# The first step of a fused linear-attention and MoE kernel: loads by two queues, half chunks staggered, y cleared by TensorE

## The chip, the cores and the metric

The kernel runs on one NeuronCore of one Trainium2 chip. The metric is the time of one execution on the device, in microseconds (us). Engines are named as the profile names them: PE (TensorE; PEld is its weight load), DVE (VectorE), ACT (ScalarE), POOL (GpSimd) and SP (SyncE, which here only issues transfers). ACT issues a few transfers too.

## What is computed

Two blocks are chained. The first is an RWKV-6 attention with a decay for each channel and token; the second is a feed-forward block with the gate h * erf(softplus(h)).

```python
# r, k, v, w: (B, H, S, D) = (4, 8, 768, 48); u: (8, 48)
for t in range(S):
    cur = einsum('bhd,bhe->bhde', u * k_t, v_t)
    y_t = einsum('bhd,bhde->bhe', r_t, state + cur)
    state = w_t[..., None] * state + einsum('bhd,bhe->bhde', k_t, v_t)
x = y.transpose(0, 2, 1, 3).reshape(3072, 384)
h = x @ w_in                                   # 384 -> 2048
g = h * erf(maximum(h, 0) + log1p(exp(-abs(h))))
out = g @ w_out                                # 2048 -> 384
```

## The kernel before

The sequence is cut into 6 chunks of 128 tokens and the 4 batches into 2 pairs, which gives 12 steps; a step handles one chunk of two batches (called j = 0 and 1 below, or half 0 and half 1 of the step). Inside a step, heads lie in pairs on the partitions: 48 channels of one head on partitions 0 to 47 and of the other on 64 to 111, in 8 columns of 128 tokens (n = 0 to 3 belong to batch 0 and n = 4 to 7 to batch 1).

Attention inside a chunk is done by halving, on two blocks of 64 tokens. At level n (1 to 6) the products of k in the left half of each block of 2^n tokens with r in its right half are made on PE (`level_products`, the matmul at L701), into one of two pairs of PSUM banks, `pp0` and `pp1`, that take turns. `take_level` (L711 on DVE, L718 on ACT) or `take_blocks` (L732 on ACT, level 5) moves them to their places in `own`, the matrix of token pairs. `scale` (L357 for one half of step 0, L364 for a whole step) then multiplies the left halves of k and the right halves of r by the decays of the other half of their blocks, in place on DVE, so that the next level's products are right. These decays are products of w over blocks, `totals`, made on POOL at L386. So within one batch the order is: scale of level n-1, products of level n, scale of level n. A product bank is free again when its level has been taken. Level 1 also carries the token's own term: it reads `rk1`, a copy of r and k in which every second token is multiplied by u (L408 and L412 on DVE, L425 and L428 on ACT).

After level 6 k is transposed on PE (L1012) into the bank that held level 5, copied to `kT` (L1015, one half by DVE and the other by ACT), and `from_own` (L745) and `state_part` (L818) make the outputs y in PSUM and the state. `fence` (L754) is a small DVE read that separates the two passes of `from_own`. `middle` is copied (L1025 on ACT, L1026 on DVE), and `through_state` (L771) adds the part of y that comes through the state. For step 0, L786 and L792 then put y into `xT`, and the projections follow: `hidden` (L1231, w_in) and `project` (L1353, w_out).

Step 0 is `attend_first`. It has nothing else to run beside it except the first weight pieces: the weights arrive as 64-bit numbers in 16 pieces of two transfers of 384 KB each and are converted by `stages`: "l" loads (L181; it waits behind a one-element copy, L272 or L274, that times it), "b" is L289 on ACT, "r" is L297 on ACT, "h" is L306 on DVE, "o" is L319 on POOL. In later steps these stages lie between the levels. `load_second` (copy L211, transfers L181) loads r and k of step 1, and `prepare(1)` makes the `rk1` of step 1, r by ACT (L425, L428) and k by POOL (L417, L421). `wait_for` (L962) is a one-element POOL copy that keeps the totals behind a scale.

Everything from `load_first` on is in one region whose engine queues keep the order in which the code issues the instructions. An instruction that waits holds up everything behind it on its engine.

`stay_warm` (L1056) and `keep_busy` (L1065) are matmuls on the identity whose results nobody reads. Before the steps DVE clears `y`, `sums`, both product banks and `apart` (L1608 to L1614), and POOL clears the states (L1625).

Of the kernel before, what the change touches and what calls it, by code (L numbers as in the profile page):

```python
# [11 lines left out]
FP32 = mybir.dt.float32  # L12
# [5 lines left out]
P = 128  # L18
# [73 lines left out]
def kernel(  # L92
    ctx: ExitStack,
    tc: tile.TileContext,
    rkw: bass.AP,
    v: bass.AP,
# [90 lines left out]
    def load_first():  # L187
# [7 lines left out]
        )  # L195
        nc.scalar.dma_start(out=u_sb[:], in_=u)
        nc.sync.dma_start(out=t5[:, 0], in_=rkw[0][:, 0:2, b0])
        nc.sync.dma_start(out=t5[:, 1, 0], in_=rkw[0][:, 0, b1])
        nc.sync.dma_start(out=t5[:, 1, 1], in_=rkw[0][:, 1, b1])
        nc.sync.dma_start(out=ws[0][:, b0], in_=rkw[0][:, 2, b0])  # L200
        nc.sync.dma_start(out=ws[0][:, b1], in_=rkw[0][:, 2, b1])
# [165 lines left out]

    def plan_totals(s):
# [21 lines left out]
    def prepare(s):  # L390


        if s < DIRECT:
# [3 lines left out]
            parts = 1 if s else NJ  # L397
            def multiply_u(i, x):
                n = slice(i * JP // parts, (i + 1) * JP // parts)
# [3 lines left out]
                        for t in (rk1[:, x, n], in_t[:, x, n] if s else turns["first"][:, i, x])  # L403
# [3 lines left out]
                if not s and not (x and not i):  # L407
                    nc.vector.tensor_mul(  # L408
                        with_u[0], with_u[1],
                        u_sb[:, :, None].to_broadcast([P, NP, C // 2]),  # L410
                    )
                    nc.vector.tensor_copy(out=plain[0], in_=plain[1])  # L412
                    return
# [16 lines left out]
            if s < 2:  # L430
                for i in range(parts):
                    for x in range(2):
                        multiply_u(i, x)
                        yield
                return
            yield
            yield
            multiply_u(0, 0)
# [14 lines left out]
        if s < DIRECT:  # L453
            ready[s] = rk1, tots, tot
            yield
            yield
            multiply_u(0, 1)
            return
# [480 lines left out]
    def attend_first(xT):  # L939


        for _ in prepare(0):
            pass
# [3 lines left out]
        own = att.tile([P, NH, HC], FP32, name="own")  # L947
        halves = [range(j * NP, (j + 1) * NP) for j in range(NJ)]
        batch = JP * C // 2 // NJ
        pp = products([P, NE, JP, HC])  # L950
        for half in halves:
            level_products(pp, by_pair(made), 1, half)
            stay_warm(2)
        nc.scalar.copy(first[:], mask_sb[:, 0, :])
        totals(1, part=slice(0, batch))
        for j in range(NJ):
            scale(0, 1, batch=j)
        load_second(t5[:, 1, 0, NP - 1, 1:2])

        def wait_for(t):  # L960

            nc.gpsimd.tensor_copy(out=block_sb[:, 0:1], in_=t5[:, 1, 0, NP - 1, t : t + 1])  # L962

        wait_for(1)
        totals(1, part=slice(batch, 2 * batch))
        totals(2, part=slice(0, batch // 2))
        nc.vector.tensor_mul(
            own[:], pp[:].rearrange("p e n t -> p (e n) t"),
            first[:, None, :].to_broadcast([P, NH, HC]),
        )  # L970
        behind = {3: (3,), 4: (4, 5), 5: (6,)}
        for level in range(2, LOG):
            pp = turns.pop("pp", None) or products([P, NE, JP, HC])
            for j, half in enumerate(halves):
                level_products(pp, first_pair, level, half)
                scale(0, level, batch=j)
            turns["pp"] = products([P, NE, JP, HC])
            keep_busy(turns["pp"], (DM,))
            (take_blocks if level == MASKED else take_level)(own, pp, level)
# [12 lines left out]
            if level == 3:  # L992
                stages["l"](1, ready[0][1][level][:, 0:1])
# [813 lines left out]
```

## Time and profile before

| what | value |
|---|---|
| time, median of 3 runs | 570.8 us (570.66 to 571.3) |
| time of the profiled execution | 571.11 us |
| its span on the core | 569.3 us |
| PE busy | 561.7 us, 99% of the span |
| DVE, ACT, POOL busy | 449.6, 359.2, 245.7 us |
| step 0, start of the span to the first matmul of `hidden(0)` | 0 to 26.44 us |
| granted PE clock in every stretch asked for | 1.00 |

The span is the part that the profile sees; 1.8 us of the execution's time lie around it. A timeline line reads: start, length, engine, source line, operation, output<-input, shape, count, and in brackets how long the engine was idle before it and what released it. A line with a count merges neighbours, so its length is that of the whole run of them. A line of a table by stretches gives the stretch, its length, then busy time and number of instructions of PE, PEld, DVE, ACT and POOL, the granted PE clock, the share of the DMA engines and GB/s.

### The profile page before, as it was taken

The numbers are of one execution on the slowest core, as the hardware profiler recorded it, in microseconds if no ns is written. First come the engines' busy times: TensorE is split into PE (matmuls) and PEld (weight loads), VectorE is DVE, ScalarE is ACT, GpSimd is POOL, SyncE is SP. The second block draws the span as 40 slices with busy tenths as digits, with TensorE's granted clock in tenths as the row PEclk, the third lists the DMA queues.
The fourth block names the chain that finished last, engine by engine and source line by source line (L and its number), as shares of the span: only waits on it lengthen the run. The fifth ranks groups of instructions, "written<-read, shape, count | busy, mean of one in ns | idle before, by whom it ended". The sixth has DMA issues, their size and how long they took to land.

```text
span 569.3 us, 16709 instructions
## 1 busy us (share of the span) xinstructions
PE 561.7 (99%) x7318; PEld 500.2 (88%) x7318; DVE 449.6 (79%) x508; ACT 359.2 (63%) x495; POOL 245.7 (43%) x264
## 2 busy tenths in 40 slices
PE   8999999999999999999999999999999999999997
PEld 6788886688998998998998998898899899989997
DVE  8774886999899898799789689689688487477730
ACT  4668787655458858747756765766676771589500
POOL 3775481632885883383484175176073000000000
PEclk9999999999999999999999999999999999999999
DMA  8794762350435325155145236235332201000000
GB/s 272 241 355 161 249 200 86 151 162 3 147 80 174 109 74 155 33 166 164 31 143 181 39 123 200 39 112 167 48 112 84 47 9 36 2 2 1 28 29 28
DMA packets 54081, 63.24 MB, mean 111 GB/s; under 512 B 35160, under 2 KB 40568, under 8 KB 52984
## 3 DMA queue, kind: packets, MB, share of 16 engines
q1 hardware_dynamic: 53480, 61.98, 34.7%
q8 instruction: 57, 0.93, 0.7%
q10 hardware_dynamic: 528, 0.20, 0.1%
q14 instruction: 16, 0.13, 0.1%
HBM read 52.39 MB, written 8.69 MB: 107 GB/s over the span
## 4 chain that ended last, share of the span: by engine, by line
PE 77%; DVE 7%; issue 3%; POOL 1%; ACT 1%; DMA 0%; ACTq 0%; POOLq 0%
PE m L1353 33%; PE m L1231 27%; PE c L1456 6%; PE pp L701 3%; PE m L1263 2%; PE y L745 2%; DVE in L364 2%; PE y L771 1%; PE pp L818 1%; POOL w_out_sb L1294 1%; DVE h L1196 1%; DVE sums L569 1%; PE c L1353 0%; DVE words L503 0%; DMA xT<-y 0%
## 5 line engine op out<-in xcount | busy, mean ns | idle before, releaser
L1231 PE MATMUL m<-xT,w_in_sb 128*128 128x256 f32 x960 | 214.6, 381 | 0.4 <-ACT h L1240 0.2
L1231 PEld LDWEIGHTS m<-xT,w_in_sb 128*128 128x128 f32 x960 | 180.1, 190 | 25.5 <-issue 0.6
L364 DVE TENSOR_TENSOR in<-in,tot_sb 128x1024 f32<-128x1024 f32 (+1 forms) x55 | 75.3, 1370 | 8.9 <-PE pp L701 6.5
L1240 ACT COPY h<-m 128x512 f32<-128x512 f32 x80 | 46.3, 580 | 52.6 <-PE m L1231 52.2
L1353 PE MATMUL m<-mixed,h 128*128 128x192 f32 x320 | 56.7, 331 | 0.0
L1353 PE MATMUL m<-w_out_sb,h 128*128 128x192 f32 x320 | 56.1, 329 | 0.0
L1353 PEld LDWEIGHTS m<-mixed,h 128*128 128x128 f32 x320 | 51.8, 190 | 0.8
L1353 PEld LDWEIGHTS m<-w_out_sb,h 128*128 128x128 f32 x320 | 52.0, 190 | 0.5
L1353 PE MATMUL m<-w_out_sb,room 128*128 128x192 f32 x288 | 49.7, 326 | 0.0
L1353 PEld LDWEIGHTS m<-w_out_sb,room 128*128 128x128 f32 x288 | 47.3, 190 | 0.1
L503 POOL TENSOR_TENSOR words<-words,own 128x384 f32<-128x384 f32 x21 | 30.4, 1447 | 25.7 <-DVE words L534 13.0
L1191 ACT ACT_TABLE_LOAD x28 | 35.9, 1283 | 8.7 <-DVE h L1196 6.7
L701 PEld LDWEIGHTS pp<-in 48*48 48x48 f32 (+4 forms) x2368 | 30.1, 120 | 10.9 <-issue 6.0
L544 POOL TENSOR_TENSOR words<-words 128x384 f32<-128x384 f32 x28 | 38.7, 1410 | 0.0
L496 POOL TENSOR_TENSOR own<-rest 128x384 f32<-128x384 f32 x7 | 8.1, 1156 | 69.2 <-PE y L745 35.1
L1187 ACT ACT_TABLE_LOAD x28 | 35.9, 1283 | 1.8 <-issue 1.3
L701 PE MATMUL pp<-in 48*48 48x32 f32 (+4 forms) x2368 | 33.9, 206 | 0.3 <-DVE in L364 0.3
L448 POOL TENSOR_TENSOR tot_sb<-tot_sb 128x256 f32<-128x256 f32 (+4 forms) x50 | 31.6, 632 | 3.8
L569 DVE TENSOR_REDUCE sums<-rk 128x16 f32<-128x768 f32 (+2 forms) x31 | 31.4, 1023 | 0.0
L544 POOL TENSOR_TENSOR rk<-words 128x384 f32<-128x384 f32 x28 | 30.6, 1121 | 0.0
L1187 ACT ACTIVATE room<-h 128x1024 f32<-128x1024 f32 x28 | 29.6, 1057 | 0.3
L319 POOL TENSOR_TENSOR w_out_sb<-w_out_sb,rest 128x768 int32<-128x768 int32 x8 | 18.1, 2264 | 21.7 <-DVE w_out_sb L311 21.5
(218 smaller groups left out, 1008.1 us busy)
## 6 DMA issues: line engine op xcount, KB each, us to landing
in<-in_rkw SPq DMA_DIRECT2D x8, 1024.0 KB, 5.1
words<-in_moe_w_in SPq DMA_DIRECT2D x16, 384.0 KB, 5.6
words<-in_moe_w_out SPq DMA_DIRECT2D x16, 384.0 KB, 4.6
words<-in_rk_rows SPq DMA_DIRECT2D x8, 768.0 KB, 6.6
w<-in_rkw SPq DMA_DIRECT2D x11, 512.0 KB
v<-in_v SPq DMA_DIRECT2D x12, 384.0 KB, 5.6
out<-o SPq DMA_DIRECT2D x23, 192.0 KB, 4.1
in<-in_rkw SPq DMA_DIRECT2D x7, 512.0 KB, 5.8
```

What stands on the lines that cost most here:

```text
L364: nc.vector.tensor_mul(halves, halves, view(tots[level - 1], 0, [[1, n], [2, nb], [0, half]]))
L448: nc.gpsimd.tensor_mul(new, pair[:, :, 0], pair[:, :, 1])
L503: engine.tensor_mul(to, to, of[:, :, None, :].to_broadcast([P, NEAR // 2 // half, half, D]))
L544: engine.tensor_mul(to[:, i], r[:, half:], k[:, part * rows + i, None].to_broadcast([P, half, D]),)
L569: nc.vector.tensor_reduce(out=to, in_=of, axis=mybir.AxisListType.X, op=ALU.add)
L701: nc.tensor.matmul(to, lhsT=rk(1, n)[rows(e), s0 : s0 + m], rhs=right, start=True, stop=True,)
L1187: nc.scalar.activation(sp_room, chunks[0], AF.Softplus)
L1191: nc.scalar.activation(at, sp_room, AF.Erf)
L1231: nc.tensor.matmul(ps[:, ff, :], lhsT=w_in_sb[:, g * FG + f + ff, kk * P : (kk + 1) * P], rhs=xT[:, kk, :], start=kk == 0, stop=kk == KT - 1,)
L1240: nc.scalar.copy(h[:, f : f + FT, :], ps[:])
L1353: nc.tensor.matmul(to, lhsT=a[:, f], rhs=b[:, f], start=start and f == 0, stop=f == FG - 1, skip_group_check=True,)
L1456: nc.tensor.matmul(to[:, f], lhsT=turns["weights"][b][:, i * FT + f], rhs=turns["tokens"][a], start=a + b in STARTS and not f, stop=True, ...
```

## The change

Only step 0 and what stands before it are touched. The host also gives r, k and w of step 0 in an order that puts the two batches one after the other (`in_rkw_first`), so that a partition's r and k of one batch are one piece of 4 KB where they were two of 2 KB.

- First loads: r and k of batch 0 are loaded in two halves of 64 partitions, one by SP's queue and one by ACT's, followed on ACT's by `u`. Then SP loads w of batch 0, r and k of batch 1 in one transfer (two before), w of batch 1 and the masks.
- Before the steps: `load_first` moves into the ordered region, `y` is no longer cleared by DVE, `sums` and `apart` are cleared by POOL, and `stay_warm` runs 4 matmuls where it ran 6.
- Copies and products with u: r by DVE and k by ACT for both batches (before, k of batch 1 was DVE's too).
- Order: batch 0 runs one level ahead of batch 1. Level 1's products (`next_tokens`) are made after level 2's, and go to the two PSUM banks of the projections (`near`), so level 2 can start without them; `take_next_tokens` moves them in two DVE instructions before level 2 is taken.
- The matmuls that nobody reads between levels (L1065, and L1056 beside level 1) go. `clear_y` takes their places: 9 matmuls of 128 columns of zeros, which clear y.
- `scale_last` replaces the scale of level 6: k's halves first, for both batches, and r's only for the second 64 tokens of a chunk, after k's.
- Stages of the first weight piece: "l" is placed after the first total, "b" and "r" come after step 1's product with u on ACT (before them, earlier), and both "h" come ahead of the fence (one on each side before). The loads of the pieces 1 and 2 and of step 1's w wait behind other elements.

```diff
+        for queue, part in ((nc.sync, slice(0, EP)), (nc.scalar, slice(EP, P))):
+            queue.dma_start(out=t5[part, 0], in_=rkw_first[part, 0, 0:2])
         nc.scalar.dma_start(out=u_sb[:], in_=u)
-        nc.sync.dma_start(out=t5[:, 0], in_=rkw[0][:, 0:2, b0])
-        nc.sync.dma_start(out=t5[:, 1, 0], in_=rkw[0][:, 0, b1])
-        nc.sync.dma_start(out=t5[:, 1, 1], in_=rkw[0][:, 1, b1])
-        nc.sync.dma_start(out=ws[0][:, b0], in_=rkw[0][:, 2, b0])
-        nc.sync.dma_start(out=ws[0][:, b1], in_=rkw[0][:, 2, b1])
+        nc.sync.dma_start(out=ws[0][:, b0], in_=rkw_first[:, 0, 2])
+        nc.sync.dma_start(out=t5[:, 1], in_=rkw_first[:, 1, 0:2])
+        nc.sync.dma_start(out=ws[0][:, b1], in_=rkw_first[:, 1, 2])
         nc.sync.dma_start(out=mask_sb[:], in_=masks)
...
+    def scale_last(batch, k):
+
+        half, nb = 1 << (LOG - 1), JP * C // NJ >> LOG
+        t, tots = turns["first"][:, batch], ready[0][1]
+        at, every, of = (NP * C, 1, 1) if k else (half + HC, NC, 2)
+        halves = view(t, at, [[2 * half * every, nb // every], [1, half]])
+        nc.vector.tensor_mul(
+            halves, halves,
+            view(tots[LOG - 1], 2 * batch * nb + of, [[2 * every, nb // every], [0, half]]),
+        )
...
+        def plain(i):
+            to, of = every_second(i, 1, 0)
+            nc.scalar.copy(to, of)
+            to, of = every_second(i, 0, 1)
+            nc.vector.tensor_copy(out=to, in_=of)
+        def times_u(i):
+            to, of = every_second(i, 0, 0)
+            nc.vector.tensor_mul(to, of, u_sb[:, :, None].to_broadcast([P, NP, C // 2]))
+            to, of = every_second(i, 1, 1)
+            for p in range(NP):
+                nc.scalar.mul(out=to[:, p], in_=of[:, p], mul=u_sb[:, p : p + 1])
+        near = [ps_m.tile([P, NP * C], FP32, name="m") for _ in range(NE)]
+        near = [t[:].rearrange("p (n t) -> p n t", t=HC) for t in near]
...
+        def clear_y(times=2):
+            to = y[:].rearrange("p e q j t -> p (e q j) t")
+            zeros = states[1][0][:].rearrange("p n d -> p (n d)")[:, :C]
+            for _ in range(times):
+                nc.tensor.matmul(
+                    to[:, cleared["of"] % (NE * NP)], lhsT=ident[:], rhs=zeros,
+                    start=True, stop=True, skip_group_check=True,
+                )
+                cleared["of"] += 1
...
+        plain(0)
+        times_u(0)
+        scale(0, 1, batch=0)
+        level(pp, 2, 0)
+        next_tokens(0)
+        wait_for(0, 1)
+        totals_of(0, 1)
+        stages["l"](0, t5[:, 1, 1, NP - 1, C - 1 : C])
+        totals_of(0, 2)
+        clear_y(1)
+        plain(1)
+        times_u(1)
+        scale(0, 2, batch=0)
+        later_pp = products([P, NE, JP, HC])
+        level(later_pp, 3, 0)
+        scale(0, 1, batch=1)
+        level(pp, 2, 1)
+        next_tokens(1)
+        clear_y()
         nc.scalar.copy(first[:], mask_sb[:, 0, :])
...
         load_second(t5[:, 1, 0, NP - 1, 1:2])
+        nc.sync.dma_start(out=vt[:], in_=v[0])
+        wait_for(1, 1)
+        totals_of(1, 1, 2)
+        scale(0, 3, batch=0)
+        scale(0, 2, batch=1)
+        level(later_pp, 3, 1)
+        clear_y()
+        take_next_tokens()
+        take_level(own, pp, 2)
+        wait_for(1, 0, 2)
+        totals(3, 4, 5)
+        second = prepare(1)
+        next(second)
+        stages["b"](0, 0)
+        stages["b"](0, 1)
+        scale(0, 3, batch=1)
+        stages["l"](1, t5[:, 1, 0, NP - 1, 4:5], True)
+        stages["r"](0)
+        pp, later_pp = later_pp, products([P, NE, JP, HC])
+        level(later_pp, 4, 0)
+        scale(0, 4, batch=0)
+        level(later_pp, 4, 1)
+        clear_y()
+        take_level(own, pp, 3)
+        scale(0, 4, batch=1)
+        wait_for(1, 0, 8)
+        totals(6)
+        nc.gpsimd.tensor_copy(out=ws[1][:, 0, 0:1], in_=block_sb[:, 0:1])
+        nc.sync.dma_start(out=ws[1][:], in_=rkw[1][:, 2])
+        pp, later_pp = later_pp, products([P, NE, JP, HC])
+        level(later_pp, 5, 0)
+        scale(0, 5, batch=0)
+        level(later_pp, 5, 1)
+        clear_y()
+        take_level(own, pp, 4)
+        scale(0, 5, batch=1)
+        take_blocks(own, later_pp, 5)
         totals = plan_totals(1)
+        pp = products([P, NE, JP, HC])
+        for i in range(NJ):
+            level(pp, LOG, i)
+            scale_last(i, True)
         take_level(own, pp, LOG)
+        wait_for(0, 1)
+        stages["l"](2, block_sb[:, 0:1])
+        wait_for(1, 1)
         next(second)
+        for i in range(NJ):
+            scale_last(i, False)
...
         stages["h"](0)
+        stages["h"](0)
         fence()
-        stages["h"](0)
...
-    nc.vector.memset(y[:], 0.0)
-    nc.vector.memset(sums[:], 0.0)
...
-        stay_warm(6)
+        load_first()
+        stay_warm(4)
+        for t in banks:
+            nc.vector.memset(t[:], 0.0)
+        nc.gpsimd.memset(apart, 0.0)
```

The loop over levels 2 to 5 that this replaces is in the listing above.

## The prediction

> **What bounds the kernel now.** I read the table by stretches first, then the timeline of step 0, then the transfers.
>
> ```profile
> 5.00:10.60 5.60, 5.37 (x134) 3.99 (x133) 4.99 (x13) 2.34 (x8) 2.19 (x5) 1.00 0.97 318
> 10.60:19.60 9.00, 7.94 (x292) 5.24 (x284) 8.74 (x13) 5.69 (x13) 3.83 (x11) 1.00 0.77 253
> ...
> 26.40:60.00 33.60, 33.60 (x754) 27.89 (x746) 20.86 (x22) 24.70 (x42) 21.75 (x24) 1.00 0.66 239
> 60.00:569.30 509.30, 505.29 (x5956) 455.41 (x5954) 407.80 (x449) 321.11 (x423) 209.47 (x205) 1.00 0.31 95
> ```
>
> From 26.4 us PE never stops, so whatever moves the first projection matmul moves the end by as much; the change touches only what lies ahead. There, from 10.6 to 19.6, DVE is busy 8.74 of 9.00 us: it sets step 0, not PE.
>
> ```profile
> 5.00 1.08 ACT L425 ACTIVATE rk<-in,u_sb 128x64 f32<-128x64 f32 x4 [2.29 <-DMA in<-in_rkw]
> 5.00 0.43 DVE L408 TENSOR_TENSOR rk<-in,u_sb 128x256 f32<-128x256 f32 x1
> ...
> 7.09 1.71 DVE L357 TENSOR_TENSOR in<-in,w 128x512 f32<-128x512 f32 x2
> ...
> 9.06 0.81 SPq L181 DMA_DIRECT2D in<-in_rkw  x2
> ...
> 13.76 1.32 ACT L425 ACTIVATE rk<-in,u_sb 128x128 f32<-128x128 f32 x4 [1.24 <-DMA in<-in_rkw]
> ...
> 16.88 1.49 ACT L732 COPY own<-pp 16x256 f32<-16x256 f32 x4 [1.24 <-PE pp L701]
> ...
> 18.28 1.32 DVE L357 TENSOR_TENSOR in<-in,tot_sb 128x512 f32<-128x512 f32 x2 [0.24 <-POOL block_sb L962]
> ...
> 18.62 1.18 ACT L718 COPY own<-pp 32x512 f32<-32x512 f32 x2 [0.25 <-PE pp L701]
> ...
> 19.14 1.16 PE L1012 MATMUL pp<-ident,in 128*128 128x128 f32 x8 [0.59 <-DVE in L357]
> ...
> 21.00 0.48 ACT L1015 COPY kT<-pp 128x384 f32<-128x384 f32 x1 [1.21 <-DVE kT L1015]
> ```
>
> The chain: r and k of batch 0 land just before 5.0; DVE works through to 19.60; the second four transposes wait for its last scale; then the kT copies (to 21.48) and `through_state` at 23.18. ACT has slack: between its product with u (13.76) and the blocks of level 5 (16.88) it idles 1.24 us, waiting for PE. That slack is what the change spends, below.
>
> ```profile
> GB/s 0 0 0 0 0 0 0 115 98 41 206 190 288 239 206 280 337 410 434 410 393 393 393 402 393 402 419 410 325 164 10 184 111 135 332 369 406 320 344 406
> ```
>
> Slices of 0.25 us from 0. The first load (issued at 0.74) moves slowly until 4.0, then at about 400 GB/s, 0.65 us for 256 KB.
>
> **The change, part by part.**
>
> *First landing.* Early end: 0.74 + 2.1 us (issue to landing of the 16 KB transfers of `xT`) + 1.3 us (512 KB at 400 GB/s) = 4.15. No gain: 4.95. I take 4.7, nearer the upper end, because the slow first slices come with one queue's 2 KB pieces but nothing shows that pieces are the cause. Then w of batch 0 lands at 5.35, r and k of batch 1 at 6.65, w of batch 1 at 7.3.
>
> *DVE.* Clearing y (0.91) and `sums` (0.27) and `apart` (0.38) leave it, so it is free at about 3.5 instead of 4.9: worth nothing, the data comes later. k of batch 1 goes to ACT, 0.35 + 0.27 off. By start-to-start rows (product with u 0.35, copy 0.27, scale of level 1 0.69, later ones 0.61): batch 0's copy, product and first scale end at 6.21; it waits for 6.65; copy and product to 7.33, scale 2 of batch 0 to 7.95, scale 1 of batch 1 to 8.63 (8.80 now). Scale 3 of batch 0 follows to 9.35. Scale 2 of batch 1 needs POOL's totals (0.61 + 0.40), which start beside that scale. Row for such a meeting: scale 1 at 7.09 took 1.11 beside a POOL total, 0.68 without. So I let the totals wait until 9.41 and end at 10.42; without the meeting scale 2 would be 0.94 earlier. Then scale 2 to 11.1, two takes of level 1 (1.2) and that of level 2 (1.16 start to start) to 13.45, and per level two scales and a take as now (1.9) to 18.2; level 6 of batch 1 on PE 0.5, k's last scale 0.42 (256 elements, by the 0.43 row): 19.2 against 19.60. r's last scales, two of under 0.3, lie beside the transposes; in the open they would cost 0.5.
>
> *ACT.* Its one issue more and the later table load (1.28) end at 3.2, before data. Products with u, 0.41 + 1.08 for each batch, end at 8.2. The copy that releases step 1's load waits for scale 1 of batch 1: issue at 8.94 (9.06 now). From issue to ACT's start is 4.70 us now, so 13.65; the weights' first piece, issued 7.42 instead of 6.79, stands nearer ahead of it, up to 0.5 more, kept for the range. Then in order: product with u for step 1, 1.88; two "b" 0.52 + 0.54; the release copy 0.19; "r" 0.92: 17.7. Only then the blocks of level 5 (1.49): 19.2, against 18.37 now, though PE has them by 16.8. Level 6's take, 1.18: 20.4 against 19.80. Now "b" and "r" run at 9.94 to 12.5, before step 1's data; behind it, these 2.0 us fall on the path.
>
> *PE.* The matmuls that go (L1065 four times 0.91, L1056 twice 1.13) lay in gaps that DVE set: nothing. Nine clears of 128 columns, about 0.22 each (two instructions, by L1056's later 0.21 for 256 columns), stand where the next products still wait for a take: nothing, 0.45 per pair if the take were early. Level 1's products, 0.5 a batch, stay.
>
> *Tail.* Transposes need k's scales (19.2) and the bank that the blocks of level 5 free (19.2): they run 19.36 to 20.41 (19.14 to 20.30 now). kT by DVE 0.56, then ACT 0.48, with hand-overs: 21.60 (21.48 now). Both "h" before the fence put it at 22.3, where the second pass of `from_own` starts at 22.34: covered by `state_part`, 0.55 if it isn't. `through_state` comes 1.70 after kT as now: 23.3, that is 0.1 us later.
>
> *POOL and SP.* POOL's clears add 0.42 + 0.27, done by 3.9, idle until 6.3 now: nothing. The second weight piece is issued at 16.84 (15.64 now), lands 3.9 to 5.0 later, ACT needs it at 24.17: 2.3 us of cover. SP's w of step 1 queues behind it, 17.64 (18.10 now), and the third piece 19.2 (18.48 now, needed at 26.97). POOL's product for step 1 waits for k's last scale as now. The first "o" ends at 23.9 now and PE needs it at 26.44.
>
> **Sum.** +0.1 us on the profiled execution's 571.1 (span 569.3 and 1.8 around it), 571.2; the median of the runs lies 0.3 below that profile: 570.9. That is no change: 0.2% (1.1 us) is about the least that a measurement of this kernel tells.
>
> [...]
>
> **The rivals.**
> (1) *Vector engine decides, faster.* If step 1's load lands sooner, ACT is no longer last. A weight transfer of 384 KB issued at 16.05 took 3.9 us; with that and first data at 4.15 ACT frees the bank at 17.9, and if POOL's totals find a gap, DVE ends at 17.7: kT at 20.3, -1.2 us, 569.6. Without the gap -0.9. For it: DVE sheds work in any case and ACT's order is the only brake. Against: the load queues closer behind the weights.
> (2) *Half-rate first load, slower.* Each half of 64 partitions goes at half rate: 512 KB at 200 GB/s instead of 400 adds 1.3 us to 4.95, so 6.2, and all behind it shifts: +1.6, 572.4. It decides from a first landing of 5.75 on (+1.1). For it: nothing in the trace had 64 partitions. Against: the first 2 us run at about 200 GB/s anyhow, so the halved rate may not show.
> (3) *PE slow, slower.* In the trace the first matmuls stand 0.43 us apart until about 5.1, later ones 0.21 (L1056, 12 in 4.54 us, then 4 in 1.13), at a granted clock of 1.00. If fewer matmuls in the gaps (four of 0.91 gone) bring the slow pace back, the first 3.4 us of the dense stretch run at half speed: +1.7, 572.6. Against: the longest gap on PE by my sum is 1.4 us.
> (4) *Step 1's load late, slower.* 5.5 us to landing, as its second half took, instead of 4.65: +1.0, with first data no earlier +1.2, 572.0.
>
> **Chances.** Forecast 0.38; (1), by 0.2% or more, 0.32; (2) 0.12; (3) 0.11; (4) 0.07. So faster 0.32, same 0.38, slower 0.30. The forecast's own range is 569.9 (landing 4.15 and quick load) to 571.9. The whole range takes most of (1), with its end 569.6 and 0.6 for a vector path a little shorter still, and of (2) to (4): 569.0 to 572.6, with some 0.1 left out on either side.
>
> **What would show it.** Right: ACT's blocks of level 5 start after "r", around 17.7, about 0.9 us after PE made them, and the transposes wait for ACT. Step 1's product on ACT starts near 13.65. Wrong: blocks start right behind PE (1); first DVE copy after 5.7 (2); L1231's first matmuls at 0.43 us apart (3); ACT waiting past 14.4 for step 1's data (4). In all cases the first L1231 should move by just what the end moves; a gap in PE after 26 us would refute that.

## The result, and the profile after

The changed kernel takes 576.73 us (median of 4 runs, 575.72 to 578.12), the kernel before 570.82 us beside it: 1.0104 times as long, with a 95% interval of 1.0081 to 1.0126. That is 5.9 us slower; the forecast was no change. The profiled execution took 577.03 us with a span of 575.2 us, against 571.11 and 569.3. One execution of the runs below, 581.78 us with the change's loads in the old kernel, counts as a slow run (the others of that kernel took 571.98 to 576.62) and is left out of its median.

In the changed file the lines have moved: `level_products` is L703 (L701 before), `scale` L358, `scale_last` L375, the transposes L1101, the kT copy by ACT L1104, `through_state` L773, `hidden` L1320, `stay_warm` L1145, and `clear_y` L1003; in the kernels tried they lie a few lines off. One matmul of `stay_warm` is two instructions in the profile, and the matmuls at the start are counted as there: 8 in the changed kernel, 12 before. The table by stretches of the changed kernel, columns as in the one of before:

```profile
5.00:10.60 5.60, 1.77 (x50) 1.31 (x52) 2.06 (x6) 2.93 (x11) 1.30 (x4) 0.87 0.59 194
10.60:19.60 9.00, 9.00 (x231) 7.96 (x223) 6.40 (x9) 1.88 (x6) 2.34 (x8) 0.50 0.74 251
...
32.60:60.00 27.40, 27.40 (x577) 22.95 (x572) 17.81 (x19) 20.24 (x35) 20.87 (x23) 1.00 0.80 288
60.00:575.20 515.20, 511.35 (x6145) 460.20 (x6136) 411.90 (x453) 325.34 (x430) 210.72 (x206) 1.00 0.31 94
```

From 10.60 to 19.60 PE is now busy for all 9.00 us and DVE for 6.40, where it was 7.94 and 8.74: the engine that sets step 0 has changed. PE also did less there, 231 matmuls instead of 292, at a granted clock of 0.50. The clock records of the trace say when that began: full clock was granted at 5.77 us, just behind the 8 matmuls at the start (they end at 5.46), taken back at 9.18, just ahead of the first products (9.29), and granted again at 26.25 only. From 5.00 to 10.60 PE was busy for 1.77 of the 5.60 us. The last two rows look like those of before, so what was lost was lost in step 0. The timeline of step 0 of the changed kernel:

```profile
1.38 0.86 ACTq L199 DMA_DIRECT2D u_sb<-in_u  x1
...
6.28 0.30 DVE L968 COPY rk<-in 128x256 f32<-128x256 f32 x1 [2.44 <-DMA in<-in_rkw_first]
7.44 1.07 ACT L976 ACTIVATE rk<-in,u_sb 128x64 f32<-128x64 f32 x4 [0.73 <-DMA u_sb<-in_u]
7.44 0.43 DVE L973 TENSOR_TENSOR rk<-in,u_sb 128x256 f32<-128x256 f32 x1 [0.86 <-DMA u_sb<-in_u]
8.54 0.69 DVE L358 TENSOR_TENSOR in<-in,w 128x512 f32<-128x512 f32 x1 [0.68 <-ACT rk L976]
9.29 1.08 PE L703 MATMUL pp<-in 48*62 48x32 f32 x32 [3.83 <-DVE in L358]
...
11.93 1.88 PE L703 MATMUL pp<-in 48*60 48x32 f32 x64
...
17.91 1.30 ACT L428 ACTIVATE rk<-in,u_sb 128x128 f32<-128x128 f32 x4 [5.81 <-DMA in<-in_rkw]
...
23.09 1.49 ACT L734 COPY own<-pp 16x256 f32<-16x256 f32 x4 [1.53 <-DVE own L713]
24.64 1.85 PE L1101 MATMUL pp<-ident,in 128*128 128x128 f32 x8 [0.27 <-ACT own L734]
27.19 0.48 ACT L1104 COPY kT<-pp 128x384 f32<-128x384 f32 x1 [1.42 <-DVE kT L1104]
29.37 0.66 PE L773 MATMUL y<-in,middle 48*48 48x64 f32 x32 [0.28 <-DVE middle L1115]
...
32.63 2.86 PE L1320 MATMUL m<-xT,w_in_sb 128*128 128x256 f32 x12
```

Three things stand in these lines. The first data are there at 6.28, `u` at 7.44, and the first scale, which waits for ACT too, ends at 9.23, 3.0 us later than forecast (6.21). PE idled 3.83 us in front of its first products. And these products are slow: 32 of them take 1.08 us and 64 take 1.88. For comparison, two groups of 64 such products in the timeline of the kernel before:

```profile
9.81 1.11 PE L701 MATMUL pp<-in 48*62 48x32 f32 x64
...
11.69 1.08 PE L701 MATMUL pp<-in 48*60 48x32 f32 x64
```

`through_state` starts at 29.37 instead of 23.18, 6.2 us later, and the first projection matmul at 32.63 instead of 26.44, 6.2 later; the span is 5.9 longer.

### The profile page after: what moved, and what is told of

The parts are those of the page before. It is cut to its first block, busy times and chain, and to the rows that moved or that the text cites. A ratio compares the mean times of both kernels' runs of the same rounds, so it can differ in the third digit from the quotient of the medians.

```text
span 575.2 us, 16709 instructions
## 1 busy us (share of the span) xinstructions
PE 564.9 (98%) x7316; PEld 505.2 (88%) x7316; DVE 449.0 (78%) x506; ACT 360.1 (63%) x501; POOL 245.4 (43%) x266
## 4 chain that ended last, share of the span: by engine, by line
PE 83%; DVE 4%; ACT 1%; issue 0%; DMA 0%; ACTq 0%
PE m L1442 33%; PE m L1320 30%; PE c L1545 6%; PE m L1352 4%; PE pp L703 4%; PE y L747 2%; PE y L773 2%; PE pp L820 1%; DVE in L365 1%; DVE h L1285 1%; PE pp L1230 1%; PE c L1442 0%; DMA xT<-y 0%; DVE sums L571 0%; PE pp L833 0%
## 5 line engine op out<-in xcount | busy, mean ns | idle before, releaser
L1320 PE MATMUL m<-xT,w_in_sb 128*128 128x256 f32 x960 | 214.7, 381 | 0.5 <-ACT h L1329 0.3
L1320 PEld LDWEIGHTS m<-xT,w_in_sb 128*128 128x128 f32 x960 | 180.0, 190 | 25.8 <-issue 0.8
L703 PEld LDWEIGHTS pp<-in 48*48 48x48 f32 (+4 forms) x2368 | 33.2, 130 | 13.5 <-issue 7.0
L703 PE MATMUL pp<-in 48*48 48x32 f32 (+4 forms) x2368 | 37.1, 215 | 3.8 <-DVE in L358 3.8
```

The lines of the kernel that those rows point to most:

```text
L703: nc.tensor.matmul(to, lhsT=rk(1, n)[rows(e), s0 : s0 + m], rhs=right, start=True, stop=True,)
L1320: nc.tensor.matmul(ps[:, ff, :], lhsT=w_in_sb[:, g * FG + f + ff, kk * P : (kk + 1) * P], rhs=xT[:, kk, :], start=kk == 0, stop=kk == KT - 1,)
```

## The experiments: the late first data

Two causes stand side by side, the late data and the slow pace, and each can hide the other. The first four runs change loads only. "After" and "before" name the kernel that a diff starts from; each time stands beside runs of the kernel before on the same chip.

**One transfer instead of two halves** (after).

```diff
-        for queue, part in ((nc.sync, slice(0, EP)), (nc.scalar, slice(EP, P))):
-            queue.dma_start(out=t5[part, 0], in_=rkw_first[part, 0, 0:2])
         nc.scalar.dma_start(out=u_sb[:], in_=u)
+        nc.sync.dma_start(out=t5[:, 0], in_=rkw_first[:, 0, 0:2])
```

> The changed kernel with r and k of batch 0 loaded by SP in one transfer of 128 partitions (still 4 KB pieces) and u first and alone on ACT's queue. Theory 'halves': the slow first landing (6.28) comes from the two transfers of 64 partitions, so it goes back to about 5.0, the first scale ends near 7.2 instead of 9.23, and the PE gap before the first products falls from 3.8 us to about 1.8. If that gap was what halved the clock, the clock stays up too: 571 to 572. Theory 'pieces': 4 KB pieces or the new order are slow as such: landing stays at 6.2, only u's 0.7 to 0.9 is won: about 576. If the halved clock has another cause than the gap: 574 to 575.

Measured: 574.54 us (573.85 to 575.35), 1.0061 of before [1.0046, 1.0076]. The timeline of this run:

```profile
4.86 0.30 DVE L967 COPY rk<-in 128x256 f32<-128x256 f32 x1 [1.01 <-DMA in<-in_rkw_first]
...
6.29 0.69 DVE L357 TENSOR_TENSOR in<-in,w 128x512 f32<-128x512 f32 x1 [0.80 <-ACT rk L975]
...
7.03 1.08 PE L702 MATMUL pp<-in 48*62 48x32 f32 x32 [1.57 <-DVE in L357]
...
26.97 0.66 PE L772 MATMUL y<-in,middle 48*48 48x64 f32 x32 [0.28 <-DVE middle L1114]
```

The same 512 KB, in the same 4 KB pieces, are there at 4.86 instead of 6.28, and `u`, alone on ACT's queue, is no longer waited for. This holds beyond one execution: in the eight profiles taken of kernels with one transfer the first copy starts at 4.50 to 5.33, in the three with the changed kernel's own loads at 5.38, 5.53 and 6.28. The scale still waits 0.80 us for ACT, whose product with u reads the k that the scale overwrites. `through_state` comes 2.4 us sooner. The products stay at 1.08 us for 32 although PE idled only 1.57 us: the pace is a cause of its own.

**`u` ahead of the half** (after), and **two full transfers**, r by SP and k by ACT, `u` ahead (after).

```diff
+        nc.scalar.dma_start(out=u_sb[:], in_=u)
         for queue, part in ((nc.sync, slice(0, EP)), (nc.scalar, slice(EP, P))):
             queue.dma_start(out=t5[part, 0], in_=rkw_first[part, 0, 0:2])
-        nc.scalar.dma_start(out=u_sb[:], in_=u)
```
```diff
+        nc.scalar.dma_start(out=u_sb[:], in_=u)
+        for queue, x in ((nc.sync, 0), (nc.scalar, 1)):
+            queue.dma_start(out=t5[:, 0, x], in_=rkw_first[:, 0, x])
-        for queue, part in ((nc.sync, slice(0, EP)), (nc.scalar, slice(EP, P))):
-            queue.dma_start(out=t5[part, 0], in_=rkw_first[part, 0, 0:2])
-        nc.scalar.dma_start(out=u_sb[:], in_=u)
```

> The changed kernel with u issued first on ACT's queue, before its half of the load; the halves stay. Theory 'halves': r and k still land near 6.2, but the products with u start at once: the first scale ends 0.7 to 0.8 earlier than 9.23, near 8.5; PE's gap is 3.0 us, so the clock may or may not fall. 576.0 if it falls, about 573 if it doesn't. Theory 'u': u's place alone made the whole delay of the first scale: its end near 7.2.

> The changed kernel with two queues kept, but cut by tensor and not by partition: SP loads r and ACT loads k of batch 0, each over all 128 partitions, u first on ACT's queue. Theory 'halves': the 64 partitions were the trouble, so both land at 5.0 or a little earlier and the run equals the one with one load, or beats it by up to 0.4. Theory 'two queues': two queues at once were the trouble; landing near 6.2 and the time near that with the halves and u first.

Measured: 575.69 us, 1.0074 [1.0056, 1.0091], and 575.66 us, 1.0083 [1.0064, 1.0101]. With `u` ahead the halves are there at 5.60 (ACT's is issued 0.42 us later for it) and the first scale ends at 7.71. With two full transfers, the timeline says:

```profile
4.08 0.30 DVE L968 COPY rk<-in 128x256 f32<-128x256 f32 x1 [0.24 <-DMA in<-in_rkw_first]
...
6.87 0.69 DVE L358 TENSOR_TENSOR in<-in,w 128x512 f32<-128x512 f32 x1 [2.16 <-ACT rk L976]
```

r alone, by SP, is in use at 4.08, the earliest of all runs; but the scale waits 2.16 us for ACT, whose k came by its own queue, and ends at 7.56, against 6.98 with one transfer. So it isn't only the cut at 64 partitions: the part on ACT's queue comes last either way (with halves, by the packets in the trace, SP's is through at 3.5 to 3.8 us and ACT's at 4.7 to 4.9, in all five profiles), and a second queue brought nothing. In neither run did the first projection matmul come sooner than in the changed kernel (33.27 and 32.65 against 32.63), though the first scale ended 1.5 and 1.7 us sooner: by the clock records they had the full pace from 31.89 and 30.91 only.

How much of the changed kernel's delay is `u`'s shows in another execution with the same loads, that of the run with the pace alone, further down:

```profile
5.53 0.29 DVE L968 COPY rk<-in 128x256 f32<-128x256 f32 x1 [2.01 <-DMA in<-in_rkw_first]
...
8.54 0.69 DVE L358 TENSOR_TENSOR in<-in,w 128x512 f32<-128x512 f32 x1 [0.68 <-ACT rk L976]
```

r and k are in use 0.75 us sooner than in the changed kernel, `u` is there at 7.44 in both, and the first scale starts at 8.54 in both. So it is `u`, behind the half, that sets the first scale; with `u` ahead, halves instead of one transfer cost 0.7 us (7.71 against 6.98).

**The change's loads alone** (before).

```diff
+        for queue, part in ((nc.sync, slice(0, EP)), (nc.scalar, slice(EP, P))):
+            queue.dma_start(out=t5[part, 0], in_=rkw_first[part, 0, 0:2])
         nc.scalar.dma_start(out=u_sb[:], in_=u)
-        nc.sync.dma_start(out=t5[:, 0], in_=rkw[0][:, 0:2, b0])
...
+        nc.sync.dma_start(out=ws[0][:, b0], in_=rkw_first[:, 0, 2])
+        nc.sync.dma_start(out=t5[:, 1], in_=rkw_first[:, 1, 0:2])
+        nc.sync.dma_start(out=ws[0][:, b1], in_=rkw_first[:, 1, 2])
```

> The kernel before with only the change's first loads: two halves of 64 partitions by two queues, u behind ACT's half, pieces of 4 KB. All else as before, its matmuls in the gaps too. Theory 'halves': first data at 5.4 to 6.3 instead of 5.0 and u at 6.2 to 7.4, where every first product with u stands: 1.3 to 2.4 us more, 572.4 to 573.5. Theory 'only the clock': under 0.5 us more, 571.0 to 571.5.

Measured: 573.54 us, 1.0043 [1.0021, 1.0065]. The timeline:

```profile
6.50 0.43 DVE L409 TENSOR_TENSOR rk<-in,u_sb 128x256 f32<-128x256 f32 x1 [1.60 <-DMA u_sb<-in_u]
...
24.66 0.67 PE L772 MATMUL y<-in,middle 48*48 48x64 f32 x32 [0.28 <-DVE middle L1027]
```

The first product comes 1.50 us later than before (6.50 against 5.00) and `through_state` 1.48 later: in the old order the loads' delay goes through to the end of the step. The median is 2.4 us above before, which is more than the trace shows. PE kept its pace here.

## The experiments: the pace of TensorE

**The old kernel without the matmuls that nobody reads** (before): those between levels and those beside level 1 gone, 8 at the start instead of 12; and **without those between levels alone** (before).

```diff
-            stay_warm(2)
...
-            keep_busy(turns["pp"], (DM,))
...
-        stay_warm(6)
+        stay_warm(4)
```
```diff
-            keep_busy(turns["pp"], (DM,))
```

> The kernel before with only the matmuls that nobody reads cut down: 4 at the start instead of 6, none beside level 1 and none between the levels. Theory 'clock': PE stays at the pace of its first matmuls (0.43 us for 256 columns), the products of a level and batch take 1.0 instead of 0.5, DVE waits for them at every level, and step 0 gets 2.5 to 3.5 us longer: 573.5 to 574.5. Theory 'they only fill gaps' (mine in the prediction): 571, no change.

> The kernel before without the four matmuls of 384 columns between the levels, but with its 6 matmuls at the start and 2 after each half of level 1. Theory 'start': what brings PE to full pace is the stretch without a gap until 6.2, and gaps of under 1 us later don't lose it: 571.0 to 571.3. Theory 'gaps': the pace is lost between the levels: 573 or more.

Measured: 573.61 us, 1.0040 [1.0028, 1.0053], and 574.54 us, 1.0059 [1.0036, 1.0082]. Both profiles are of the slowest execution of their kernel (575.33 and 579.13 us), so they show the loss at its largest; the fastest executions (571.86 and 571.62) lost under 0.8 us. The timeline of the first:

```profile
8.30 1.93 PE L701 MATMUL pp<-in 48*62 48x32 f32 x64
...
18.69 1.94 PE L1010 MATMUL pp<-ident,in 128*128 128x128 f32 x8 [0.50 <-DVE in L357]
```

64 products take 1.93 us (1.11 before) and the eight transposes 1.94 (1.16), and this at a granted clock that the profile gives as 1.00 throughout. The view prints 1.00 where the trace has no clock record yet; the first record, at 30.40, is the moment when the pace came. With the 12 matmuls at the start kept and only the gaps opened it came, and went again. The second kernel's PE by stretches of 1 us (busy, matmuls, granted clock, DMA share, GB/s):

```profile
12.00:13.00 1.00, 0.80 (x47) 1.00 1.03 413
13.00:14.00 1.00, 0.44 (x32) 1.00 1.02 401
14.00:15.00 1.00, 0.45 (x20) 0.71 0.36 142
15.00:16.00 1.00, 1.00 (x56) 0.50 0.13 35
```

Its longest wait between levels is 1.11 us. The pace went in the second of two half-idle microseconds (at 14.41 by the record; PE busy for 0.44 and 0.45 us of them). Such a wait doesn't always cost the pace: five other profiles of this case have one of 1.0 to 1.1 us between levels and keep 1.00 behind it. What decides is not shown.

These two runs take only cover away from the old kernel, and cost 2.5 and 3.3 us: the matmuls that go were no filling.

**Curing the pace with narrow matmuls**: after, with 26 matmuls at the start instead of 8 and four clears of 128 columns at each place; and the kernel with one transfer, with 16 and the same clears.

```diff
-        def clear_y(times=2):
+        def clear_y(times=4):
-        clear_y(1)
+        clear_y(4)
-        stay_warm(4)
+        stay_warm(13)
```
```diff
-        stay_warm(4)
+        stay_warm(8)
```

> The changed kernel with its loads, but PE kept busy: 13 matmuls instead of 4 before the first products, which last until about 9.2, and four clears of y where there were one or two. Theory 'clock': the granted clock stays at 1.00, the products of a level and batch take 0.5 us instead of 1.0, and step 0 gets about 3 us shorter: 573.5 to 574. Theory 'loads only': the low clock lies beside DVE's work and costs nothing; 576.5 or more.

> The changed kernel with both cures: one transfer for r and k of batch 0 with u alone on ACT's queue, and PE kept busy, by 8 matmuls at the start (4 in the change; they end near 7.0, when the first products can start) and four clears of y each time. Theory 'load and clock': the products of a level and batch take about 0.65 us from start to result instead of 1.08, through_state starts at 23 to 24 (29.4 in the changed kernel, 23.2 before), and the time is 571 to 572, the kernel before's; nothing of the change's saving on DVE is left. Theory 'the order itself is worse': through_state later than 24.5, above 572.5. If the low clock comes after step 0, as with 13 matmuls, 576.

Measured: 582.73 us, 1.0208 [1.0193, 1.0223], and 577.03 us, 1.0105 [1.0076, 1.0133]. Both are slower than what they were to cure. The products were fast (0.66 us for 32), and although the 26 matmuls held the first of them until 10.41, `through_state` starts at 27.81 and 25.69, 1.56 and 1.28 us sooner than in the kernels to cure. The time was lost behind it: the first projection matmul starts at 34.26 and 31.81, 1.6 us later than in those, and the list of PE's waits has entries that neither the kernel before nor the changed one has. Of the first, then of the second:

```profile
PE pp L820 <- issue: 1.6, 1, 1.6
PE m L1320 <- DMA xT<-y: 1.6, 1, 1.6
PE y L747 <- issue: 1.0, 1, 1.0
PE pp L703 <- issue: 0.7, 2, 0.5
```
```profile
PE pp L702 <- issue: 2.5, 2, 1.3
...
PE m L1319 <- DMA xT<-y: 1.6, 1, 1.6
PE y L746 <- issue: 0.9, 1, 0.9
```

"Issue" is time in which the profile shows nothing that PE waited for. The granted clock fell too, from 28.11 to 34.94 us in the first run and from 28.73 to 32.14 in the second, by the records.

**Curing it with wide matmuls**: 16 at the start, and one clear of 384 columns in place of two of 128. Once with the changed kernel's own loads, once with one transfer.

```diff
-        def clear_y(times=2):
+        def clear_y(times=1):
-            to = y[:].rearrange("p e q j t -> p (e q j) t")
-            zeros = states[1][0][:].rearrange("p n d -> p (n d)")[:, :C]
+            to = y[:].rearrange("p e q j t -> p e (q j t)")
+            zeros = states[1][0][:].rearrange("p n d -> p (n d)")
+                e, second_part = divmod(cleared["of"] % (2 * NE), 2)
-                    to[:, cleared["of"] % (NE * NP)], lhsT=ident[:], rhs=zeros,
+                    to[:, e, second_part * C : second_part * C + DM], lhsT=ident[:], rhs=zeros,
-        stay_warm(4)
+        stay_warm(8)
```

> The changed kernel with its own first loads (halves, u behind one of them) and its own order, and only the cure of TensorE's pace: 16 matmuls on the identity at the start instead of 8, and the clearing of y by one matmul of 384 columns at each place instead of two of 128. Theory 'two causes that add': the first scale still runs from about 8.5 to 9.2 us, the 32 products of a level take 0.66 us instead of 1.08, through_state starts near 27.2 us (29.37 with the slow pace, 24.9 with the pace and the landing cured), and the time is 576.7 less about 2, some 574.7 us. Rival 'landing alone': the pace hid behind the late data, the time stays at 576 us or more although the products are fast. Rival 'pace lost again': TensorE idles past the end of the 16 matmuls at 8.4 us and the products take 1.08 us all the same: through_state after 29 us, 576.5 us.

> The changed kernel with one first load, 8 matmuls at the start, and y cleared by one matmul of 384 columns at each of its five places (0.91 us, two instructions) instead of one to four of 128 columns. Theory 'instruction supply': the 1.0 to 1.3 us that PE waited for issue in the middle of groups with four narrow clears come from too many short instructions, so they vanish, and PE keeps full pace through step 0 and after it: through_state at 24.0 to 24.5, 571.5 to 572.5. Theory 'any filler': the waits stay, through_state near 25.7, 575 to 577.

Measured: 574.75 us, 1.0065 [1.0051, 1.0079], with the old loads, and 574.36 us, 1.0067 [1.0040, 1.0095], with one transfer. The timeline of the first:

```profile
9.29 0.65 PE L703 MATMUL pp<-in 48*62 48x32 f32 x32 [1.79 <-DVE in L358]
...
26.39 0.66 PE L773 MATMUL y<-in,middle 48*48 48x64 f32 x32 [0.28 <-DVE middle L1116]
```

Its first products start at 9.29, as in the changed kernel, and `through_state` comes 2.98 us sooner: that is what the pace cost. By the start of `through_state`, one transfer alone is worth 2.40 us (26.97), the pace alone 2.98 (26.39) and both 4.48 (24.89) of the 6.19; they overlap by 0.9. In the medians, less of it shows: both together stand 3.1 us above before. The profiled execution of that kernel has one "issue" wait of 1.1 us on PE between 40 and 60 us, which takes a part back.

## The experiments: what is left

**The order on ACT** (from the kernel with one transfer and wide clears): "b", "b" and "r" ahead of step 1's product with u, as before the change. Then, on top of it, **the plain copy of k of batch 0 by DVE** instead of ACT.

```diff
+        stages["b"](0, 0)
+        stages["b"](0, 1)
+        stages["r"](0)
         second = prepare(1)
         next(second)
-        stages["b"](0, 0)
-        stages["b"](0, 1)
         scale(0, 3, batch=1)
         stages["l"](1, t5[:, 1, 0, NP - 1, 4:5], True)
-        stages["r"](0)
```
```diff
-            nc.scalar.copy(to, of)
+            if i:
+                nc.scalar.copy(to, of)
+            else:
+                nc.vector.tensor_copy(out=to, in_=of)
```

In the kernel that these two start from, ACT does what the prediction feared: "r" ends, the blocks start right behind it, and the transposes wait for ACT.

```profile
19.40 1.47 ACT L733 COPY own<-pp 16x256 f32<-16x256 f32 x4
...
20.93 1.09 PE L1101 MATMUL pp<-ident,in 128*128 128x128 f32 x8 [0.57 <-ACT own L733]
```

> The same with wide clears, and ACT's conversions of the first weight piece (two b and r) put before its product with u for step 1, as in the kernel before; the release of the second piece after it. Theory 'ACT last' (the prediction's chain): 2.0 us leave ACT's path, the blocks of level 5 start about 1.5 us earlier and through_state about as much: near 22.8 to 23.2, 570.0 to 571.0. Theory 'DVE last': less than 0.3 us better than with wide clears alone.

> The same as with the conversions moved, and the plain copy of k of batch 0 made by DVE instead of ACT, so that ACT's reads of k, which the first scale must not overtake, end earlier. Theory 'first scale waits for ACT's reads': the first scale starts 0.3 us earlier, near 6.0, and the time falls by 0.3. Otherwise no change or 0.2 more.

Measured: 573.33 us, 1.0038 [1.0024, 1.0051], and 573.0 us, 1.0035 [1.0023, 1.0048]. ACT's order moves `through_state` by 0.10 us (24.89 to 24.79) and the copy by 0.16, but that is the start and not the edits: the first products start when the 16 matmuls end, at 8.33, 8.21 and 8.05 in the three kernels, and from there to `through_state` it is 16.56, 16.58 and 16.58 us. With ACT's old order the transposes wait for DVE's last scale at the same place (20.82), so neither edit was worth anything in the trace. The medians fall by 1.0 and 0.3, but their intervals overlap. The timeline of the better one:

```profile
8.05 0.66 PE L702 MATMUL pp<-in 48*62 48x32 f32 x32
...
14.92 1.13 PE L702 MATMUL pp<-in 48*56 48x32 f32 x64 [1.09 <-DVE own L712]
...
24.63 0.66 PE L772 MATMUL y<-in,middle 48*48 48x64 f32 x32 [0.28 <-DVE middle L1118]
```

`through_state` is still 1.45 us later than before. The 16 matmuls hold the first products until 8.05, though the first scale ended at 6.49, and DVE idles 1.71 us ahead of its second scale.

**Shorter warm-ups** (from that kernel): 12 matmuls at the start, 10, and 12 with one more wide clear where PE idles 1.09 us.

```diff
-        stay_warm(8)
+        stay_warm(6)
```
```diff
-        stay_warm(8)
+        stay_warm(5)
```
```diff
-        stay_warm(8)
+        stay_warm(6)
         level(later_pp, 3, 1)
-        clear_y()
+        clear_y(2)
```

> The kernel with one load, wide clears, the old order on ACT and DVE's copy, but with 12 matmuls on the identity at the start instead of 16. There the 16 ran until 8.12 us, while the first scale had ended at 6.49, and DVE then waited 1.71 us for the first level's products before its second scale at 8.84. Theory 'warm-up too long': the 12 end near 7.2 us, the first products start at 7.1 instead of 8.05, DVE's chain and through_state move up by 0.9 (24.63 to 23.7), and the time falls from 573.0 to about 572.1 us. Rival 'DVE's order': what DVE does between 10.7 and 14.7 us (products with the next tokens and a predicated copy of 1.34 us between two scales) sets the end, the start doesn't matter: through_state within 0.2 of 24.6, time 572.8 to 573.2 us. Rival 'pace': 12 matmuls don't hold the pace and the 32 products take 0.9 us or more: 573.5 us or more.

> As the kernel with 12 matmuls at the start, with 10 of them. Theory 'warm-up too long': they end near 6.2 us, before the first scale does at 6.5, so the first products start at 6.6, at most 0.5 us earlier than with 12, partly at the slow pace (0.7 to 1.1 us for 32); through_state near 23.4 us, 571.6 to 572.1 us. Rival 'pace': the matmuls from the start are too few and the products of the first levels take 1.08 us: through_state 25 us or later, 573.5 us or more. Rival 'DVE's order': 572.8 to 573.2 us.

> The kernel with 12 matmuls at the start, and beside them one more 384-column matmul that clears y, in the place where TensorE idles 1.03 us between the third and the fourth level's products (from 12.7 to 13.7 us); its result is the same zeros. With 12 and no filling the products started 1.5 us earlier than with 16, but the granted clock fell to 0.5 between about 16 and 23 us and through_state started no earlier (24.96 against 24.63). Theory 'idle stretches cost the pace': with the gap filled the clock stays at 1.00, level 5 takes 1.15 instead of 1.45 us and the transposes 1.09 instead of 1.94, through_state starts near 23.5 us, the time is 572.0 us, 1 below the kernel with 16. Rival 'too short a warm-up': the pace falls all the same, since the 12 matmuls and not the gap decide: through_state 24.5 us or later, 573.5 to 575 us. Rival 'instruction supply': the pace holds in the profile, but TensorE stands for about 1.1 us on nothing that the profile shows, and the time stays above 573 us.

Measured: 574.44 us, 1.0058 [1.0042, 1.0073]; 575.55 us, 1.0076 [1.0052, 1.0100]; 576.12 us (573.13 to 577.03), 1.0096 [1.0079, 1.0113]. All three missed: none is faster than the kernel with 16. In the first, the products started 1.48 us earlier, at 6.57, and fast; then PE by stretches of 1 us shows this:

```profile
15.00:16.00 1.00, 0.86 (x15) 1.00 0.46 181
16.00:17.00 1.00, 1.00 (x60) 0.50 0.09 26
...
22.00:23.00 1.00, 1.00 (x35) 0.59 0.74 215
```

The pace was gone for 6.8 us (16.00 to 22.83 by the records), and `through_state` starts at 24.96. In the second it holds until an "issue" wait, and falls in it (at 23.87; 0.50 from 25 to 30 us). Up to there this run tells what the long warm-up cost: its transposes start at 19.75, 0.91 us sooner than with 16 matmuls (20.66) and still 0.61 later than before the change (19.14). In the third it holds to the end of the step, but PE stands twice on "issue". Timeline of the second, then of the third:

```profile
24.14 1.00 PE L746 MATMUL y<-own,v 64*48 64x64 f32 x28 [1.16 <-issue]
```
```profile
23.82 0.24 PE L819 MATMUL pp<-v,kT 64*48 64x48 f32 x2 [0.59 <-issue]
...
28.42 0.39 PE L702 MATMUL pp<-rk 48*64 48x64 f32 x10 [0.35 <-issue]
```

The pace held in the profiled execution with the gap filled, as its theory had it, but five profiles without the filling held it behind such a gap too, so this doesn't show that the filling did it. That execution took 573.13 us and the median is 3 us above it. What the other executions lost isn't in any trace. So a part stays open: the executions of one of these three kernels lie 3 to 5 us apart, those of the kernel before beside them within 1.7.

The "issue" waits have something in common. The profile names two DMA queues "instruction"; the larger moves 57 packets of 16 KB (58 in one run). Eleven times, in six profiles, PE stands on "issue" for 0.35 us or more in the middle of a group of equal matmuls, and each time the wait ends 1.29 to 1.52 us behind the end of such a packet (24.14 behind 22.78, 23.82 behind 22.37, 28.42 behind 27.04 in the three lines above), though the packets come about 5 us apart (4.2 to 7.7 us between 14 and 63 us in the changed kernel). That PE waits there for its next instructions is an estimate from these distances alone: no run changed how they are loaded, and why it happens in some executions only isn't shown. Nothing here beats the kernel before.

## Why the prediction was wrong

- **First landing (4.7, bounds 4.15 to 4.95).** The term failed: 6.28. The upper bound "no gain" was wrong, since the row it came from was of one queue and 128 partitions. Rival (2) had the landing right (6.2) and its mark, a first DVE copy after 5.7, is there. That is in part luck: two other profiles with the same loads have 5.38 and 5.53, and the load did not run at half rate. By the packets its 512 KB took 2.8 us (2.13 to 4.95) against 2.6 with one transfer (1.77 to 4.34). A stretch at about 200 GB/s there is, from 4.0 to 5.5 us (361 to 397 with one transfer), but by 4.0 over four fifths of the load were through. The rest of the delay lies between the last packet and the first copy, 1.3 us against 0.5, and what it waited for is not shown. Two halves brought no gain: in every profile they were later than one transfer, by 0.05 to 1.8 us between the nearest and the farthest of them (first copy at 5.38 to 6.28 against 4.50 to 5.33).
- **"Batch 0's copy, product and first scale end at 6.21."** This left out two waits (and the rows it names add up to 6.01). `u` is issued third, after ACT's half, and is there at 7.44, 6.06 us after its issue; I had it in time without costing its place in the queue. And the scale overwrites the k that ACT's product with u reads, 0.68 us more (0.80 with one transfer); by the prediction's own terms for ACT, 0.41 and 1.08 behind 4.7, that product ends at 6.19, so no scale could end at 6.21. Both could be read from the diff. They make the 3.0 us by which the first scale is late: the landing is hidden behind `u`, since r and k at 5.53 instead of 6.28 left the scale at 8.54.
- **"PE. The matmuls that go lay in gaps that DVE set: nothing."** This is the step that failed most. They cost nothing and held the pace: taking them out of the old kernel cost 2.5 and 3.3 us, and holding the pace in the changed one moves `through_state` by 2.98. Rival (3) had the mechanism, but put it in the dense stretch after step 0; there L1320's first 12 take 2.86 us as before, and its mark is absent. It came in step 0, where PE, at half the pace, became the bound. The argument against it (longest gap 1.4 us) fell twice: the late data made a gap of 3.83 us, in which the clock granted at 5.77 was lost, and in the old kernel a wait of 1.11 us was the longest before it fell. The nine clears were put at 0.22 us each and at nothing; at half the pace they took 5.67 us in all (0.79 for the first, 1.22 for each pair), between 11.2 and 23.4 us, where PE hardly idled. What they cost by themselves was not tried.
- **ACT's chain.** "Blocks wait for 'r'" did not decide in the changed kernel: "r" was long over and the blocks (23.09) waited 1.53 us for DVE. With loads and pace cured the chain is there as forecast, but giving ACT its old order back was worth nothing in the trace, because DVE's last scale came no sooner.
- **DVE's chain.** In the changed kernel its own work never came to decide, so rival (1) wasn't tested there. With everything cured the step is still 1.45 us longer than before. By the run with 10 matmuls at the start, 0.9 of it is the long warm-up; the other 0.6 stay at full pace, so the staggered order was no shorter there either. Which piece of it costs them isn't shown.
- **Rival (4), step 1's load late.** Its mark is there, ACT starts step 1's product at 17.91, past 14.4: the load is issued at 12.13 instead of 8.94 and takes 5.8 us instead of 4.7. But nothing waited for it in the changed kernel, as the 1.53 us of ACT ahead of the blocks show. In the run with the pace alone it did decide: there the chain that ends last runs over `u`, then this load (12.02 to 17.32) and ACT's work up to the blocks. With one transfer and wide clears the product starts at 15.85, when PE releases it.
- **The tail.** Right: `through_state` comes 1.70 us after kT (27.67 to 29.37), as forecast, and the first projection moves by 6.19 where the span grows by 5.9. No wait behind 26 us took the place of the others.

## What to carry to other kernels

A matmul whose result nobody reads may be what keeps TensorE at its full pace, as in the old kernel, which took 2.5 and 3.3 us more without some of them: before taking one out, compare the time of equal groups of matmuls (here 0.66 against 1.08 us for 32) in a run without it, and take the time of several executions, since the pace came at a different point in each here (12 matmuls at the start took 4.54 to 5.49 us). For a first load, compare one transfer over all partitions with two queues on the chip (here the first copy came at 4.50 to 5.33 us with one transfer and at 5.38 to 6.28 with two halves), and put a small operand that the first instruction needs ahead of the large one (behind the half, `u` was there at 7.44 us; ahead of it, the product with `u` started at 5.81). When two engines share a first tile, list the readers that the next write in place has to wait for, on both engines (here 0.68 us of waiting for ACT's).

## What the runs showed of the hardware that was not expected

- A printed granted clock of 1.00 is not yet the pace: in the old kernel without its extra matmuls it reads 1.00 from 5 to 20 us while 64 products take 1.93 instead of 1.11 us. In that trace the clock records begin only where full clock is first granted, at 30.40 us (at 23.72 with one transfer, 5.11 in the kernel before), and the views print 1.00 ahead of that. The spacing of equal matmuls tells: the first matmuls of the kernel before stand 0.43 us apart until 5.11, later ones 0.21.
- A busy PE did not bring the pace back by itself here: in the changed kernel PE was busy for all of the 9.00 us from 10.60 to 19.60, and the clock stayed at half for 17.07 us. The clock stayed in one state for 3.41 and 17.07 us there, and for 10.24 and 6.83 with 12 matmuls at the start; the three longer times are 5.0, 3.0 and 2.0 times the first.
- The same 12 matmuls at the start took 4.85 us in one execution and 5.49 in another: the pace came at a different point each time. With 8 of them it came in two of five profiles (4.58 and 5.77 us) and was gone again at 7.99 and 9.18; in the other three it came at 23.72, 30.40 and 30.91.
- A transfer of 2 KB (`u`) issued behind half of the first load was in use 6.06 us after its issue, and with r and k, 256 KB each, on two queues, r by SP's was in use at 4.08 and k by ACT's, issued 0.45 us later, only at 5.45.
- In the profiles of six of the kernels tried PE stands on "issue" for 0.35 to 1.6 us in the middle of a group of equal matmuls, in those of the kernel before, of the changed one and of the rest it doesn't. All eleven waits end 1.29 to 1.52 us behind the end of a 16 KB instruction packet; in one of them the clock fell (at 23.87 us), and behind two (at 28.11 and 28.73).
